# A linear-attention layer with a GELU MLP on one core: two loads under way from the fourth on, and a planner that reckons with 235 bytes per ns

## The chip, the cores and the metric

The kernel runs on one core of a Trainium2 chip. The metric is device time in microseconds (us) of one execution. Engines are named as the profile names them: PE is TensorE (PEld its weight loads), DVE is VectorE, ACT is ScalarE, POOL is GpSimd, SP is SyncE, which issues every DMA here.

## What is computed

An RWKV-like recurrence over 768 tokens, for 4 batches and 8 heads of size 48, followed by an MLP with GELU (384 to 2048 to 384) on the 3072 tokens.

```
for t in range(S):
    cur = einsum('bhd,bhe->bhde', u[None] * k[:, :, t], v[:, :, t])
    y[:, :, t] = einsum('bhd,bhde->bhe', r[:, :, t], state + cur)
    state = w[None, :, :, None] * state + einsum('bhd,bhe->bhde', k[:, :, t], v[:, :, t])
x = y.transpose(0, 2, 1, 3).reshape(B * S, H * D)
h = x @ w_in
out = (0.5 * h * (1 + erf(h / sqrt(2)))) @ w_out
```

## The kernel before

**Tiling.** The tokens are cut into 6 chunks of 128. In a chunk, two heads make a pair, so that there are 24 groups (chunk, pair), worked on one after the other, four to a chunk. The recurrence of a group becomes matrix products: scores of keys and queries (L473, into the PSUM buffer A), what the group adds to the state (the gains, L484, into UE), and the readout from the old state and from the group itself (L492 and L510, into Y). The result is split into a high and a low half (L573 on ACT, L574 on DVE) into xx, the input of the MLP, or x for the pair that comes first and is spread over the three others (L523). The MLP of a chunk is 16 steps, one for each block of 128 hidden units: three times three products into Hp (L657), GELU (L687), split into gh and gl (L688, L689), nine products into O (L700). 96 steps in all.

**Loads.** A group needs T (r and k with the head dimension on partitions, L252 and L254, 448 or 384 KB; from the third group on in two halves of 48 rows) and N (k and v by token, L261, 384 KB). T is multiplied by powers of the decay on DVE (L434), N on POOL (L441). The first four groups have buffers of their own, T0 to T3 and N0 to N3; the later ones take turns in Tb and Nb. The 16 blocks of weights (768 KB each, L372) land in three buffers raw in turn and are split into wh and wl in six passes on ACT and DVE (L387 to L400). All that happens in the first lap over the blocks; later chunks find the weights in place.

**What holds a load back.** Loads go through `in_turn` (L227), which keeps only so many of them under way. It makes each load wait, on SP, until the load `back` places before it in the list `landing` has landed. SP issues in order, so whatever stands behind a waiting load waits too.

```
back = UNDERWAY + (len(landing) < START)
behind = landing[-back] if first is not None and len(landing) >= back else None
```

The first thirteen stand in `LOADS`: t0, t1, n0, t2, n1, t3, w0, n2, n3, w1, t4, w2, n4, where t is T, n is N and w is a block of weights.

**The planner.** The kernel writes no order by hand. Each operation is added to a `Plan` (L52) with its engine, a duration, a due time, and what it reads and writes. `Plan.run` (L89) then steps through model time, picks the ready operation with the earliest due time on each engine, and emits it; each engine executes in the order emitted. A load of n bytes is reckoned as n / RATE ns on a bus that carries one load at a time, 1050 ns after its issue and 940 ns before its landing is seen.

```
if e == "sp":
    free[e] = start + 640
    bus = max(bus, start + 1050) + ns / RATE
    end = bus + 940
```

**Fillers.** Where the planner sees TensorE waiting in the prologue, it fills the gap with products of zeros that nobody reads (`heat`, L314, all recorded at L315): wide ones of 512 columns into UE or A, narrow ones of 256 columns into AE. How many are emitted follows from the gap in model time:

```
for _ in range(int(share * (start - free[e]) / ns)):
    fill()
```

They are ordinary instructions of TensorE's stream, and run whether the data came sooner or later than in the model. From the first group of the second chunk on none is emitted.

Of the kernel before, what the change touches and what calls it, by code (L numbers as in the profile page):

```python
# [34 lines left out]
WMIN, WMAX = 0.7, 1.25  # L35
NT = 8
NEAR = 8
RATE = 270.0
LATER = 10 ** 7
FIRST, STEP, STEP_LAST = 23000, 8400, 3900  # L40
WEIGHT_AHEAD, GROUP_AHEAD, GROUP_DUE = 12500, 28000, 20000
HEATS, SMALL, HEAT_NS, HEAT_ROOM = 7, 26, 400, 300
LOADS = ("t0", "t1", "n0", "t2", "n1", "t3", "w0", "n2", "n3", "w1", "t4", "w2", "n4")
UNDERWAY, START = 2, 10
URGENT, WORTH = 1000, .5
LEEWAY, SHARE = 700, 0.9
BARE = 2
# [4 lines left out]
class Plan:  # L52
# [26 lines left out]
    def time(self, n):  # L79
        e, ns = self.ops[n][:2]  # L80
        return 2200 + ns / RATE if e == "sp" else ns

# [6 lines left out]
    def run(self):  # L89
# [14 lines left out]
        for _ in self.ops:  # L104
# [28 lines left out]
# [4 lines that stand above are left out]
# [823 lines left out]
```

## Time and profile before

| what | us |
|---|---|
| three timed runs | 487.2, 490.36, 490.95 |
| their median | 490.36 |
| the profiled execution | 487.44 |
| its span, first to last instruction | 485.6 |
| TensorE busy in the span | 477.3 |
| VectorE, ScalarE, GpSimd busy | 266.0, 176.3, 63.7 |

How to read it: the profile is of one execution, whose own time is the span and some 2 us around it. Busy time is an average over a prologue of some 30 us (loads, masks, the first four groups), a first lap with the splitting of the weights, and the rest, where only the groups and the MLP run. A stage's limit is read from that stage.

### The profile page before, as it was taken

The numbers are of one execution on the slowest core, as the hardware profiler recorded it, in microseconds if no ns is written. First come the engines' busy times: TensorE is split into PE (matmuls) and PEld (weight loads), VectorE is DVE, ScalarE is ACT, GpSimd is POOL, SyncE is SP. The second block draws the span as 40 slices with busy tenths as digits, with TensorE's granted clock in tenths as the row PEclk, the third lists the DMA queues.
The fourth block names the chain that finished last, engine by engine and source line by source line (L and its number), as shares of the span: only waits on it lengthen the run. The fifth ranks groups of instructions, "written<-read, shape, count | busy, mean of one in ns | idle before, by whom it ended". The sixth has DMA issues, their size and how long they took to land.

```text
span 485.6 us, 11783 instructions
## 1 busy us (share of the span) xinstructions
PE 477.3 (98%) x5150; PEld 387.7 (80%) x5150; DVE 266.0 (55%) x432; ACT 176.3 (36%) x355; POOL 63.7 (13%) x85
## 2 busy tenths in 40 slices
PE   8899999999999999999999999999999999999996
PEld 5788778888887887888888878888888887888885
DVE  7888977983654556535536536545544422322223
ACT  6588978843122134222232331331431311211111
POOL 4200000002202202202022122022021100000000
PEclk9999999999999999999999999999999999999999
DMA  8776676331311312312302403113403000100002
GB/s 215 229 248 247 202 219 215 112 93 66 83 45 51 93 45 89 108 35 60 93 20 74 148 1 93 44 51 94 136 12 93 1 12 13 65 1 0 0 1 70
DMA packets 13193, 42.25 MB, mean 87 GB/s; under 512 B 2160, under 2 KB 2544, under 8 KB 13136
## 3 DMA queue, kind: packets, MB, share of 16 engines
q1 hardware_dynamic: 13136, 41.43, 28.4%
q8 instruction: 42, 0.69, 0.6%
q14 instruction: 15, 0.12, 0.1%
HBM read 34.74 MB, written 4.72 MB: 81 GB/s over the span
## 4 chain that ended last, share of the span: by engine, by line
PE 96%; DMA 1%; DVE 1%; issue 1%; SPq 0%; DVEq 0%
PE Hp L657 42%; PE O L700 41%; PE A L473 3%; PE Y L492 3%; PE Y L510 2%; PE Y L484 1%; PE AE L315 1%; PE Y L700 1%; DMA T<-in_rkT_dram 1%; PE Y L523 0%; DVE Am L559 0%; PE UE L484 0%; DVE wa L873 0%; DVE T L434 0%; PE A L315 0%
## 5 line engine op out<-in xcount | busy, mean ns | idle before, releaser
L657 PE MATMUL Hp<-xx,wh 128*128 128x512 f32 x576 | 166.7, 397 | 0.0
L687 ACT ACTIVATE gf<-Hp 128x512 f32<-128x512 f32 x96 | 57.4, 598 | 231.3 <-PE Hp L657 225.5
L688 DVE CAST gh<-gf 128x512 fp32r<-128x512 f32 x95 | 45.4, 478 | 170.8 <-ACT gf L687 170.0
L657 PEld LDWEIGHTS Hp<-xx,wh 128*128 128x128 f32 x576 | 106.8, 188 | 24.9 <-ACT gf L687 0.4
L657 PE MATMUL Hp<-xx,wl 128*128 128x512 f32 x288 | 83.3, 396 | 0.0
L700 PE MATMUL O<-gh,wh 128*128 128x512 f32 (+1 forms) x285 | 81.9, 394 | 0.0
L700 PE MATMUL O<-gh,wl 128*128 128x512 f32 (+1 forms) x285 | 80.9, 390 | 0.5 <-issue 0.5
L700 PE MATMUL O<-gl,wh 128*128 128x512 f32 (+1 forms) x285 | 80.5, 389 | 0.0
L689 DVE TENSOR_TENSOR gl<-gf,gh 128x512 fp32r<-128x512 f32 x95 | 73.5, 774 | 9.3
L657 PEld LDWEIGHTS Hp<-xx,wl 128*128 128x128 f32 x288 | 54.0, 188 | 12.9
L700 PEld LDWEIGHTS O<-gh,wh 128*128 128x128 f32 x285 | 52.4, 188 | 12.6 <-issue 0.3
L700 PEld LDWEIGHTS O<-gh,wl 128*128 128x128 f32 x285 | 52.5, 188 | 12.5 <-issue 0.9
L700 PEld LDWEIGHTS O<-gl,wh 128*128 128x128 f32 x285 | 52.6, 188 | 11.5
L464 ACT ACTIVATE Am<-diag,cs 128x64 f32<-128x64 f32 x120 | 31.7, 338 | 27.3 <-DVE cs L459 27.3
L438 POOL TENSOR_TENSOR Nb<-Nb 128x384 f32<-128x384 f32 x15 | 15.7, 1047 | 122.3 <-DMA Nb<-in_rkv_dram 114.7
L441 POOL TENSOR_TENSOR Nb<-Nb,WN 128x384 f32<-128x384 f32 x20 | 21.0, 1048 | 50.8 <-DMA Nb<-in_rkv_dram 30.1
L434 DVE TENSOR_TENSOR Tb<-Tb,E 112x1024 f32<-112x1024 f32 x20 | 24.3, 1215 | 3.1 <-DMA Tb<-in_rkT_dram 3.1
L529 DVE SCALAR_TENSOR_TENSOR Sb<-Sa,E,Y 48x192 f32<-48x192 f32 x40 | 16.5, 413 | 14.2 <-ACT xx L573 7.7
L501 POOL MEMSET turn<- 1x1 f32 x19 | 1.7, 88 | 137.3 <-PE Y L492 137.3
L573 ACT CAST xx<-Y 112x512 fp32r<-112x512 f32 (+1 forms) x18 | 10.6, 587 | 22.9 <-PE Y L484 16.4
L559 DVE COPY_PREDICATED Am<-past,A 128x512 f32<-128x512 uint32 x24 | 17.6, 735 | 0.4
L456 POOL TENSOR_TENSOR Nb<-Nb,u_sb 128x384 f32<-128x384 f32 x15 | 17.8, 1188 | 0.1
(112 smaller groups left out, 396.8 us busy)
## 6 DMA issues: line engine op xcount, KB each, us to landing
raw<-in_wmlp_dram SPq DMA_DIRECT2D x16, 768.0 KB, 5.0
Nb<-in_rkv_dram SPq DMA_DIRECT2D x15, 576.0 KB, 3.9
Tb<-in_rkT_dram SPq DMA_DIRECT2D x40, 192.0 KB, 3.5
out_dram<-raw SPq DMA_DIRECT2D x5, 768.0 KB, 3.7
Nb<-in_rkv_dram SPq DMA_DIRECT2D x5, 384.0 KB, 3.3
xx<-x SPq DMA_DIRECT2D x30, 64.0 KB, 2.3
N<-in_rkv_dram SPq DMA_DIRECT2D x4, 384.0 KB, 5.1
T<-in_rkT_dram SPq DMA_DIRECT2D x2, 448.0 KB, 4.7
```

Of the source, the lines that this page charges most:

```text
L434: add("dve", sdve(1024), LATER if g.gi else -10 ** 5, lambda: nc.vector.tensor_tensor(out=flat, in0=flat, in1=E[:, 0, g.p].rearrange("l h ...
L438: add("pool", pool(DM), LATER, lambda: nc.gpsimd.tensor_tensor(out=g.n[:, 0], in0=g.n[:, 0], in1=g.n[:, 1], op=ALU.mult), r=[g.K], w=[g.R])
L441: it = nc.gpsimd.tensor_tensor(out=g.kn, in0=g.kn, in1=WN[:, g.p].rearrange("s j d -> s (j d)").unsqueeze(1).to_broadcast([C, NB, 2 * D]), ...
L456: add("pool", pool(DM), LATER, lambda: nc.gpsimd.tensor_tensor(out=g.n[:, 0], in0=g.n[:, 0], in1=u_sb[:, g.p, :].unsqueeze(1).to_broadcast ...
L464: add("act", sact(HALF) + 60, LATER, lambda x=x, b=b: nc.scalar.activation(out=g.am[:, x, b, :], in_=diag2, func=AF.Copy, scale=g.sums[:, ...
L529: return nc.vector.scalar_tensor_tensor(out=g.s[h + 1][quarter(1 - x)], in0=g.s[h][l], scalar=E[l, 1, g.p, h, MID:MID + 1], in1=gained(g, ...
L559: add("dve", 722, LATER, lambda: nc.vector.copy_predicated(out=g.am, mask=mask.bitcast(U32).unsqueeze(1).unsqueeze(1).to_broadcast([C, 2, ...
L657: nc.tensor.matmul(O[3], lhsT=wt[j][:, 0, k_ * 128:(k_ + 1) * 128], rhs=x[:, a, k_, :], start=start and k_ == ks[0], stop=stop and k_ == k ...
L687: add("act", 600, LATER, lambda: nc.scalar.activation(out=gf, in_=O[3], func=AF.Gelu), r=["H"], w=["gf"])
L688: add("dve", sdve2(512), LATER, lambda: nc.vector.tensor_copy(out=high, in_=gf), r=["gf"], w=[GH])
L689: add("dve", sdve(512), LATER, lambda: nc.vector.tensor_tensor(out=low, in0=gf, in1=high.bitcast(F32), op=ALU.subtract), r=["gf", GH], w=[GL])
L700: nc.tensor.matmul(bank(dst)[:, a:b], lhsT=wt[j][:, 1, d * 128:(d + 1) * 128], rhs=gt[:, a:b], start=(j == 0 and n == 0), stop=(j == NJ - ...
```

## The change

Three numbers change: START, up to which three loads may be under way, goes from 10 to 3, RATE from 270 to 235 bytes per ns; UNDERWAY stays at 2. Since the first three loads never wait, the fourth is now the first to do so, and waits for the second load and no longer for the first.

```
--- before.py
+++ after.py
@@ -35,13 +35,13 @@
 WMIN, WMAX = 0.7, 1.25
 NT = 8
 NEAR = 8
-RATE = 270.0
+RATE = 235.0
 LATER = 10 ** 7
 FIRST, STEP, STEP_LAST = 23000, 8400, 3900
 WEIGHT_AHEAD, GROUP_AHEAD, GROUP_DUE = 12500, 28000, 20000
 HEATS, SMALL, HEAT_NS, HEAT_ROOM = 7, 26, 400, 300
 LOADS = ("t0", "t1", "n0", "t2", "n1", "t3", "w0", "n2", "n3", "w1", "t4", "w2", "n4")
-UNDERWAY, START = 2, 10
+UNDERWAY, START = 2, 3
 URGENT, WORTH = 1000, .5
 LEEWAY, SHARE = 700, 0.9
 BARE = 2
```

SP issues the same loads in the same order; what they wait for moves. On SP before (DMAHW1, 2, 3 and 5 tell the landing of T0, T1, N0 and of the second half of T2):

```order
L252 DMA T1_103<-in_rkT_dram 112x1024
L261 DMA N0_110<-in_rkv_dram 128x768
L254 DMA T2_104<-in_rkT_dram 48x1024 [waits DMAHW1_49,Pool_49]
L254 DMA T2_104<-in_rkT_dram 48x1024
L261 DMA N1_111<-in_rkv_dram 128x768 [waits DMAHW2_49]
L254 DMA T3_105<-in_rkT_dram 48x1024 [waits DMAHW3_49,Pool_49]
```

And on SP after:

```order
L252 DMA T1_103<-in_rkT_dram 112x1024
L261 DMA N0_110<-in_rkv_dram 128x768
L254 DMA T2_104<-in_rkT_dram 48x1024 [waits DMAHW2_49,Pool_49]
L254 DMA T2_104<-in_rkT_dram 48x1024
L261 DMA N1_111<-in_rkv_dram 128x768 [waits DMAHW3_49]
L254 DMA T3_105<-in_rkT_dram 48x1024 [waits DMAHW5_49,Pool_49]
```

T2 waits for T1 in place of T0, N1 for N0 in place of T1, T3 for T2 in place of N0; the loads up to the tenth follow in the same manner, and from the eleventh on each waits for the same load as before.

On PE, behind the gains of the first group (the first of the three numbers in a row is the buffer: T_102 to T_105 and N_110 to N_113 belong to groups 0 to 3, AE<-zeros are narrow fillers):

```order
 L484 MATMUL UE<-N_110 48x48 x16
-L315 MATMUL AE<-zeros 128x256 x13
+L315 MATMUL AE<-zeros 128x256 x10
+L473 MATMUL A<-T_104 64x64 x16
+L473 MATMUL A<-T_104,KB_108 64x64 x16
 L492 MATMUL Y<-T_102,Sb 48x64 x8
 L510 MATMUL Y<-Am_116,N_110 48x64 x16
-L473 MATMUL A<-T_104 64x64 x16
-L473 MATMUL A<-T_104,KB_108 64x64 x16
-L484 MATMUL UE<-N_111 48x48 x16
-L315 MATMUL AE<-zeros 128x256 x11
+L315 MATMUL AE<-zeros 128x256 x12
```

The scores of group 2 move ahead of the readout of group 0, and the gains of group 1 move behind the scores of group 3. Over the whole prologue the narrow fillers go from 13 + 11 + 12 + 12 = 48 to 10 + 12 + 6 + 17 + 10 = 55. On DVE the two selects of group 1 (L559) move with this, directly behind the product of T2 (L434) and ahead of the setting of the spread matrix (L306, L307).

On PE, in the first two steps of the MLP (wh_75 and wl_83 are the two halves of the weights of step 0, wh_76 those of step 1; A<-zeros are wide fillers):

```order
 L657 MATMUL Hp<-xx_122,wl_83 128x512
 L657 MATMUL Hp<-xx_122,wh_75 128x512
-L315 MATMUL A<-zeros 128x512
+L315 MATMUL A<-zeros 128x512 x5
 L657 MATMUL Hp<-xx_122,wh_75 128x512
 L657 MATMUL Hp<-xx_122,wl_83 128x512
 L657 MATMUL Hp<-xx_122,wh_75 128x512
-L315 MATMUL A<-zeros 128x512 x3
+L315 MATMUL A<-zeros 128x512 x5
 L657 MATMUL Hp<-xx_122,wh_76 128x512 x3
```

The wide fillers there go from 1 + 3 to 5 + 5. One more wide filler, into UE, stands before the gains of the first group. Further on the planner swaps neighbours on ACT, DVE and PE: in the first lap ACT takes its three passes over block 4 (L390, L387, L393) before it makes the high half of block 3 (L398), as before, but now with its last pass over block 3 (L387) ahead of them all. POOL's order is unchanged.

## Rows read from the trace of the kernel before

**Rows 1.** The page: busy times, granted clock by slice, chain by engine.

```profile
PE 477.3 (98%) x5150; PEld 387.7 (80%) x5150; DVE 266.0 (55%) x432; ACT 176.3 (36%) x355; POOL 63.7 (13%) x85
...
PEclk9999999999999999999999999999999999999999
...
PE 96%; DMA 1%; DVE 1%; issue 1%; SPq 0%; DVEq 0%
```

**Rows 2.** Busy time by stretch: us, engines' busy us, clock, DMA share, GB/s.

```profile
34.04:160.00 125.96, 125.49 (x1580) 101.72 (x1581) 90.69 (x144) 74.03 (x123) 14.46 (x20) 1.00 0.43 134
```

**Rows 3.** Chain in order of time, 12 to 34 us: start us, us, what.

```profile
12.21 1.74 PE AE L315 x13
...
16.42 0.61 issue
...
17.73 1.51 PE AE L315 x11
...
21.36 0.70 issue
...
23.59 1.62 PE AE L315 x12
...
27.38 1.63 PE AE L315 x12
...
32.42 0.23 PE A L315
```

**Rows 4.** Timeline of SP, 5 to 36 us: start us, us, engine, what.

```profile
5.47 0.79 SPq L254 DMA_DIRECT2D T<-in_rkT_dram  x2
7.06 0.35 SPq L261 DMA_DIRECT2D N<-in_rkv_dram  x1
...
34.30 1.59 SPq L372 DMA_DIRECT2D raw<-in_wmlp_dram  x2
```

**Rows 5.** DMA issues at 5.8, 49, 7, 32.6 and 34.3 us: KB, us to landing.

```profile
T<-in_rkT_dram SPq DMA_DIRECT2D x1, 192.0 KB, 4.2
...
Tb<-in_rkT_dram SPq DMA_DIRECT2D x1, 192.0 KB, 3.3
...
N<-in_rkv_dram SPq DMA_DIRECT2D x1, 384.0 KB, 6.0
...
Nb<-in_rkv_dram SPq DMA_DIRECT2D x1, 384.0 KB, 2.9
...
raw<-in_wmlp_dram SPq DMA_DIRECT2D x1, 768.0 KB, 5.0
```

**Rows 6.** Timeline of VectorE (DVE), 10 to 16 us.

```profile
10.53 1.96 DVE L434 TENSOR_TENSOR T<-T,E 112x1024 f32<-112x1024 f32 x1
...
13.17 0.73 DVE L559 COPY_PREDICATED Am<-diag,A 128x512 f32<-128x512 uint32 x1
13.94 0.73 DVE L559 COPY_PREDICATED Am<-past,A 128x512 f32<-128x512 uint32 x1
14.56 1.21 DVE L434 TENSOR_TENSOR T<-T,E 112x1024 f32<-112x1024 f32 x1
```

**Rows 7.** DMA queues from 14.4 to 14.6 us: packets, MB, share of 16 engines.

```profile
q1 hardware_dynamic: 20, 0.05, 88.6%
q8 instruction: 1, 0.02, 33.9%
```

**Rows 8.** Timeline of ScalarE (ACT), 39 to 45 us.

```profile
39.35 0.92 ACT L390 ACTIVATE wb<-raw 128x768 uint32<-128x768 uint32 x1
...
40.96 1.07 ACT L393 ACTIVATE wb<-raw 128x768 f16<-128x768 f32 x1
41.90 0.87 ACT L387 ACTIVATE wa<-raw 128x768 f32<-128x768 f32 x1
44.06 0.83 ACT L398 CAST wh<-wa 128x768 fp32r<-128x768 f32 x1 [1.29 <-DVE wa L395]
```

**Rows 9.** Timeline of TensorE (PE) at 46.6 us, the step on block 3.

```profile
46.62 0.97 PE L657 MATMUL Hp<-xx,wh 128*128 128x512 f32 x3
```

More of the change, by code (lines that the diff above doesn't have):

```diff
@@ L37 @@
 NEAR = 8
-RATE = 270.0
+RATE = 235.0
 LATER = 10 ** 7
@@ L43 @@
 LOADS = ("t0", "t1", "n0", "t2", "n1", "t3", "w0", "n2", "n3", "w1", "t4", "w2", "n4")
-UNDERWAY, START = 2, 10
+UNDERWAY, START = 2, 3
 URGENT, WORTH = 1000, .5
```

## The prediction

> **What bounds the kernel now.** I read the page first. TensorE is busy 98% of the span and is 96% of the chain that ended last, and the granted clock stands at its upper level in all forty slices [rows 1]. Then I cut the span into stretches. From 34.04 us, where the second MLP step begins, to 160 us TensorE works 125.49 of 125.96 us [rows 2]: there is nothing to win in the lap over the sixteen weight blocks, and a load that comes later there is hidden as long as its slack lasts. The change can act in the first 34 us and, if weights come late, in that lap.
>
> The chain in order of time shows what the first 34 us are made of [rows 3]. From 12.21 us on it never leaves TensorE: scores, gains and readout of four groups, and between them products of zeros ("AE L315", "A L315"). Those are the fillers, put where the planner expected TensorE to wait: 48 of 256 columns in the chain (13, 11, 12 and 12), and 4 of 512 columns. TensorE waits for nothing that the profile names there, except that it stands still twice, 0.61 and 0.70 us, called "issue", in the middle of a batch. The fillers are thus not free: in this execution nothing arrived later than they ended, and each moves the end by its own length.
>
> **The change part by part.** *Fillers.* With loads of 235 bytes per ns and two under way the planner expects later data, and writes 55 narrow fillers in place of 48, and 10 wide ones in place of 4. A narrow one costs (1.74 + 1.51 + 1.62 + 1.63) / 48 = 0.135 us, a wide one 0.23 us [rows 3]. Seven and six of them: 0.95 + 1.38 = 2.3 us. If the data really come as late as the planner thinks, TensorE would have stood still for that time, so the price is the same either way. One more wide one, into UE, stands earlier, where VectorE's first selects are waited for; that wait hides it, and it costs 0.23 us at most if not.
>
> *T2.* Before, SP issues T2 at 5.47 us, when T0 has landed; now it waits for T1, the landing that let N1 go at 7.06 us [rows 4]. Its second half is issued some 0.4 us behind the first and took 4.2 us; a half like it took 3.3 us with less beside it, at 49 us [rows 5]. T2 so lands at 10.8 to 11.6 us, against 10.0 us. VectorE took T2 up at 10.53 us, and needed 1.96 us where the next product of the same size took 1.21 us [rows 6]. I reckon 1.2 us, and behind it the two selects of group 1, 1.5 us (13.17 us to 14.67 us in the rows), which now follow at once, with the setting of the spread matrix behind them. They free the buffer A for the scores of group 2, which TensorE now does before it reads out group 0. Ready: 13.5 to 14.4 us. TensorE comes there at 12.21 us plus ten fillers, 13.56 us. Wait: 0 to 0.9 us; I take 0.5, the middle, as both durations of a half are equally near.
>
> *What is queued behind T2 on SP.* N1 goes behind N0, T3 behind T2, the first weight block behind N1, N2 behind T3, N3 behind the block, the second block behind N2, and SP issues in this order, so each may hold the next. N1 took 6.0 us with three under way [rows 5]; issued at about 8 us it lands by 14.1 us, and its gains now stand behind the scores of group 3. T3, of the same two halves as T2, has the same bounds of 0 to 0.9 us for the scores of group 3, but twelve fillers (1.62 us) stand ahead of those; I take 0.2. The first block goes some 2 us later, and its first product comes after the last narrow fillers, which end at 29.0 us: hidden. Without that cover the chain would lengthen by those 2 us.
>
> *The two stretches of "issue".* An instruction packet of queue q8 starts 1.9 us before the first of them, beside load packets that fill the DMA engines to nine tenths [rows 7]. With two loads under way it has less to queue behind, and more fillers stand between the batches of small products that eat instructions fastest. The two could shrink to nothing, or stay: 0 to 1.31 us back, I take 0.7.
>
> The Trainium skill (Runtime: NRT & Kernel Launch, Instruction fetch mechanics) says that instructions are refilled in blocks of 256 by a queue of their own and that this is mostly hidden. By that rule there would be nothing to give back here, and the sum would be 0.7 us higher. The trace agrees that such packets come on a queue of their own, and shows 1.31 us for which it names nothing else, so I keep the term.
>
> *Weights in the first lap.* For block 3, ScalarE ends the high half at 44.06 + 0.83 = 44.89 us [rows 8] and TensorE starts the step at 46.62 us [rows 9]: 1.7 us of slack, and TensorE itself will come about 2 us later. I cost the lap at nothing; this slack is the cover, and the third rival is the price without it. It can pay 0.47 us at most, TensorE's idle time there [rows 2].
>
> **The sum** is 2.3 + 0.5 + 0.2 - 0.7 = +2.3 us. Its ends are 2.3 - 1.31 = +1.0 us, and 2.3 + 0.9 + 0.9 = +4.1 us. On the profiled execution, 487.44 us (485.6 us of it span), that is 489.7 us. The timed runs of before stand at 487.2, 490.36 and 490.95 us: the median is 2.9 us above the profiled one, and no row tells why. From the median the same sum gives 490.36 + 2.3 = 492.7 us. I put the forecast midway between the two, 491.2 us. Its own range goes from 487.44 + 1.0 = 488.4 us to 490.36 + 4.1 = 494.5 us.
>
> [...]
>
> **Rivals.** First, *the stretches of "issue" go and nothing waits*: +1.0 us, 488.4 us from the profiled execution and 491.4 us from the median, 489.9 us between. For it: the packet lies where the DMA engines are full. Against it: batches of small products now stand closer, the scores of group 2 directly before the readout of group 0.
>
> Second, *the 2.9 us between the profiled execution and the median are late loads*. The old planner reckons with 270 bytes per ns; where loads run slower, TensorE waits behind its fillers, and the new plan has that time filled already. Then after stands at 489.7 us whatever the loads do: 0.7 us below the median. Nothing in the one trace speaks for or against it; it is why the forecast is not the full 492.7 us.
>
> Third, on the other side, *the weight blocks become the bound of the first lap*: slower. ScalarE's order puts three passes of block 4 (0.92 + 1.07 + 0.87 us) ahead of the high half of block 3 (0.83 us) [rows 8], so that block 3 is ready 3.7 us behind the landing of block 4, which was at 34.30 + 5.0 = 39.3 us [rows 4, 5]. The step on block 3 would start at 46.62 + 2.3 = 48.9 us, so the mechanism decides from a landing later than 45.2 us, 5.9 us later than before. Thirteen loads stand ahead, each behind the one two places before it; in one strand of six or seven, 0.9 us lost at each handover would do it, where a lone load takes 2.9 us whole. From there each further block waits for its own load: 0.5 us a step over the remaining twelve is 6 us, half of it hidden by the three buffers, so 491.2 + 3 to 491.2 + 6, say 495.8 us. Against it: from the eleventh load on the old kernel has two under way as well, and keeps its 1.7 us.
>
> Fourth, *faster by over 1%*: 4.9 us are wanted, and all that TensorE stands still between 12 and 160 us is 1.31 + 0.47 us. No row bears it out.
>
> **How the numbers follow.** Forecast 0.52, first rival 0.20, second 0.15, third 0.10, fourth 0.03. About 1%, that is 485.5 to 495.3 us around 490.36 us, is what a measurement of this kernel can tell from no change. Forecast and the first two rivals lie inside; of the third I count 0.02 inside. So faster 0.03, within 0.89, slower 0.08. The range 488.4 to 494.5 us holds the first two rivals too, and leaves out the third and the fourth and a little at both ends.
>
> **What would show it.** Right: the second MLP step starts 1 to 4.1 us later than 34.04 us; 55 and 10 fillers stand in a chain that is still all TensorE; a wait of under 1 us before the scores of group 2, with T2 landing at 10.8 to 11.6 us; and from the second step to the end as long as before, 485.6 - 34.04 = 451.6 us. Wrong: a chain that leaves TensorE for a load between 14 and 34 us, idle time of TensorE over 1 us between 34 and 160 us, or longer stretches of "issue".

## The result, and the profile after

The changed kernel takes 497.21 us (median of six runs, 492.45 to 503.13), the kernel before 488.34 us beside it (six runs, 487.07 to 490.95): a ratio of 1.014 [1.0105, 1.0175], slower by 1.4%, and above the predicted range. The ratios here are taken from fast executions alone, so that this one leaves out the run of 503.13 us, and they are not the quotients of the medians beside them. Timed again with more runs of before on one chip (the first experiment) it was 495.36 (four runs) against 489.76 us, 1.0129 [1.0085, 1.0172].

The profiled execution is the fastest of the six, 492.45 us, with a span of 490.7 us, 5.1 us longer than before's. The page, against [rows 1]:

```profile
PE 479.9 (98%) x5164; PEld 389.9 (79%) x5164; DVE 266.3 (54%) x432; ACT 176.4 (36%) x355; POOL 63.6 (13%) x85
...
PEclk9999999999999999999999999999999999999999
...
PE 94%; DMA 3%; issue 1%; DVE 1%; SPq 0%; ACT 0%
```

TensorE has 14 matmuls more, and loads are now 3% of the chain. The chain in order of time, against [rows 3] (start us, us, what):

```profile
7.52 4.37 DMA T<-in_rkT_dram
...
12.31 4.46 DMA T<-in_rkT_dram
...
21.67 0.72 PE AE L315 x6
...
24.08 2.23 PE AE L315 x17
...
28.48 1.38 PE AE L315 x10
...
33.26 1.14 PE A L315 x5
...
35.10 1.14 PE A L315 x5
36.24 2.10 PE Hp L657 x9
```

Up to 16.8 us the chain is the loads of T, one behind the other: T2's second half lands at 7.52 + 4.37 = 11.89 us, T3's at 16.77 us. The second MLP step begins at 36.08 us (its first matmul; the chain shows it one batch later), 2.0 us later than before. TensorE's stops and waits over the whole span:

```profile
PE Y L484 <- issue: 2.7, 1, 2.7
PE A L473 <- DVE Am L559: 2.1, 3, 0.8
PE A L315 <- DVE E L338: 1.6, 1, 1.6
PE Hp L657 <- ACT gf L687: 0.3, 1, 0.3
```

The third row stands in both kernels, at the very start. The second holds the waits for T2 and T3, through VectorE's selects. In TensorE's timeline (start us, us, what, and in brackets the idle time ahead and what ended it):

```profile
14.68 0.69 PE L473 MATMUL A<-T 48*64 48x64 f32 x32 [0.78 <-DVE Am L559]
...
19.48 0.69 PE L473 MATMUL A<-T 48*64 48x64 f32 x32 [0.82 <-DVE Am L559]
...
65.19 0.52 PE L484 MATMUL Y<-Nb 64*48 64x48 f32 x26
68.43 0.30 PE L484 MATMUL Y<-Nb 64*48 64x48 f32 x6 [2.72 <-issue]
```

The two stretches of "issue" of 0.61 and 0.70 us [rows 3] are gone. In their place stands one of 2.72 us in the first lap, in the middle of a batch of small products. The lap as a stretch, against [rows 2]:

```profile
36.08:160.00 123.92, 120.88 (x1439) 97.30 (x1438) 89.51 (x141) 71.94 (x117) 14.38 (x19) 1.00 0.45 137
```

TensorE is idle for 123.92 - 120.88 = 3.04 us there, against 0.47 us before. From the second step to the end it takes 490.7 - 36.08 = 454.6 us, against 451.6 us. So of the 5.1 us, 2.0 come ahead of the second step and 3.1 behind it. Of the latter, 2.25 us are that one stop, less the 0.47 us that before stood still, and 0.3 us a wait for ScalarE (the last row of the waits above); the rest has no wait to its name.

**Where the stop stands.** Before's 0.47 us of idle time in the lap is a stop called "issue" too, at another place of the work:

```profile
65.74 0.50 PE L700 MATMUL O<-gh,wl 128*128 128x512 f32 x1 [0.47 <-issue]
```

The two look unrelated until one counts. TensorE's matmuls in stretches that end within a stop, before (the number behind x is the count):

```profile
0.00:16.60 16.60, 14.00 (x348) 10.86 (x349) 13.01 (x27) 10.26 (x23) 6.11 (x14) 1.00 0.85 230
16.60:21.60 5.00, 4.33 (x127) 3.83 (x127) 4.07 (x8) 4.08 (x7) 1.99 (x2) 1.00 0.89 273
21.60:65.50 43.90, 42.94 (x765) 35.09 (x764) 37.38 (x55) 36.77 (x55) 3.38 (x5) 1.00 0.68 225
```

And after:

```profile
0.00:67.00 67.00, 61.38 (x1240) 50.47 (x1241) 52.01 (x84) 49.42 (x80) 11.69 (x21) 1.00 0.72 222
```

Before stood still behind matmul 348, 348 + 127 = 475 and 475 + 765 = 1240; after stood still behind 1240 as well. 765 is six times 127.5. The stops are tied to the number of the instruction, not to the work: TensorE stands where its stream passes from one block of some 127 matmuls with their weight loads to the next. The 14 extra matmuls at the start push all later work 14 places on in these blocks. In before, the last block ahead of no. 1240 runs from 61.42 to 65.27 us and holds 3.85 us of work, wide matmuls among it. In after it lies wholly within the 160 small products of a group, and is through in 2.0 us, from 63.72 to 65.71 us. The DMA queues of after from 63.72 us, when that block was entered, to 66.10 us, and in the tenth of a microsecond behind it (packets, MB, share of 16 engines):

```profile
q1 hardware_dynamic: 132, 0.74, 86.7%
...
q1 hardware_dynamic: 8, 0.02, 106.9%
q8 instruction: 1, 0.02, 60.1%
```

Until 66.10 us there is no instruction packet at all, beside loads that fill the engines to 87%. It comes 2.4 us after the block was entered, when TensorE has already stood for 0.4 us, and TensorE goes on 2.3 us after it. In before the packet came 2.0 us after the block was entered, and 3.85 us of work covered all but 0.47 us (the queues from 61.42 to 63.38 us, and from there to 63.50 us):

```profile
q1 hardware_dynamic: 74, 0.45, 76.6%
...
q8 instruction: 1, 0.02, 50.4%
```

### The profile page after: what moved, and what is told of

Same layout as the page of the kernel before. It is cut to its first block, busy times and chain, and to the rows that moved or that the text cites. A ratio compares the mean times of both kernels' runs of the same rounds, so it can differ in the third digit from the quotient of the medians.

```text
span 490.7 us, 11809 instructions
## 1 busy us (share of the span) xinstructions
PE 479.9 (98%) x5164; PEld 389.9 (79%) x5164; DVE 266.3 (54%) x432; ACT 176.4 (36%) x355; POOL 63.6 (13%) x85
## 4 chain that ended last, share of the span: by engine, by line
PE 94%; DMA 3%; issue 1%; DVE 1%; SPq 0%; ACT 0%
PE Hp L657 41%; PE O L700 40%; DMA T<-in_rkT_dram 3%; PE Y L492 3%; PE A L473 3%; PE Y L510 2%; PE Y L484 2%; PE Y L700 1%; PE AE L315 1%; PE A L315 0%; PE Y L523 0%; DVE Am L559 0%; DVE wa L873 0%; DVE T L434 0%; PE UE L484 0%
## 5 line engine op out<-in xcount | busy, mean ns | idle before, releaser
L700 PEld LDWEIGHTS O<-gl,wh 128*128 128x128 f32 x285 | 52.5, 188 | 11.6
L700 PEld LDWEIGHTS O<-gh,wl 128*128 128x128 f32 x285 | 52.5, 188 | 11.6
L434 DVE TENSOR_TENSOR Tb<-Tb,E 112x1024 f32<-112x1024 f32 x20 | 24.3, 1216 | 3.4 <-DMA Tb<-in_rkT_dram 3.3
L559 DVE COPY_PREDICATED Am<-past,A 128x512 f32<-128x512 uint32 x24 | 17.7, 739 | 0.5
```

Source lines behind the costliest of these rows:

```text
L434: add("dve", sdve(1024), LATER if g.gi else -10 ** 5, lambda: nc.vector.tensor_tensor(out=flat, in0=flat, in1=E[:, 0, g.p].rearrange("l h ...
L559: add("dve", 722, LATER, lambda: nc.vector.copy_predicated(out=g.am, mask=mask.bitcast(U32).unsqueeze(1).unsqueeze(1).to_broadcast([C, 2, ...
L700: nc.tensor.matmul(bank(dst)[:, a:b], lhsT=wt[j][:, 1, d * 128:(d + 1) * 128], rhs=gt[:, a:b], start=(j == 0 and n == 0), stop=(j == NJ - ...
```

## The experiments

The theory: the time goes where a block of instructions is run through faster than the next one is fetched, and the change moved small products into such a place. The rivals: the 17 fillers and the late T2 and T3 cost it (*fillers*), or one of the two edits by itself does, by its loads. To move the places without moving anything else, the number SMALL of tiny warm-up products (L323) was changed; each is two matmul records, of about 20 ns, that feed nothing. There the planner's price of the warm-up was set to its old value, so that the plan stays word for word the same:

```
-        add("pe", 430 * HEATS + 40 * SMALL, 10, warm_up, ...
+        add("pe", 4050, 10, warm_up, ...
```

The table gathers what was measured. "Places" is by how many matmuls the work stands further on than in before. "Step 2" is where the second MLP step begins in the profiled execution, "lap on" the time from there to the end. Stops are those called "issue" of over 0.4 us, with the number of matmuls ahead of them.

| run | places | median us (before) | ratio | step 2 | lap on | stops: no. and us |
|---|---|---|---|---|---|---|
| before | 0 | 488.34 | | 34.04 | 451.6 | 348 0.61, 475 0.70, 1240 0.47 |
| after | +14 | 497.21 (488.34) | 1.014 | 36.08 | 454.6 | 1240 2.72 |
| again | +14 | 495.36 (489.76) | 1.0129 | 38.99 | 454.9 | 602 1.45, 1240 2.57 |
| after_fewer_small | 0 | 491.38 (489.76) | 1.0031 | 37.52 | 452.8 | 1240 0.68 |
| before_more_small | +14 | 491.87 (489.76) | 1.0059 | 37.37 | 452.0 | 348 0.48, 475 2.07, 602 1.18, 1240 0.95 |
| start_only | +2 | 489.34 (489.76) | 1.0016 | 35.63 | 451.3 | 348 0.58 |
| rate_only | +4 | 493.02 (489.52) | 1.0084 | 37.77 | 453.3 | 602 1.10, 1240 1.38 |
| after_half_fillers | 0 | 490.92 (489.52) | 1.0039 | 34.27 | 457.4 | 348 0.43, 1240 3.35 |
| after_small14 | -10 | 491.12 (489.52) | 1.0059 | 35.86 | 455.1 | 348 0.67, 984 2.67 |
| before_small21 | -10 | 489.31 (489.52) | 1.0005 | 33.14 | 451.0 | none |
| start_small32 | +14 | 491.27 (489.7) | 1.0036 | 37.05 | 452.9 | 368 1.99, 475 0.44, 1240 1.37 |
| rate_small24 | 0 | 492.02 (489.7) | 1.0031 | 38.54 | 452.7 | 475 0.49, 602 1.01, 1240 0.70 |
| after_small33 | +28 | 494.99 (489.7) | 1.0095 | 40.45 | 453.3 | 1496 1.51 |
| before_half_fillers | -10 | 490.23 (488.42) | 1.0031 | 35.84 | 451.5 | 984 0.41 |

Of these 26 stops, 25 stand on the ladder, and each of the 25 ends 2.2 to 2.8 us after the start of an instruction packet in its own trace. The one behind no. 368 does not: the last such packet started 5.3 us before it ended. "Step 2" needs care: in six of the profiles (start_only, rate_only, after_fewer_small, rate_small24, after_small33, before_half_fillers) TensorE's products go at a slower pace until 10 to 17 us, in the other eight only until 5 to 6 us (*Other places* below).

### The changed kernel again, and its places moved back

`again` is the changed kernel unaltered.

> The changed kernel once more, unaltered, for a second profile. Theory of the instruction blocks: TensorE stands still for about 2.7 us at its matmul 1240, near 68 us, as in the first profile, and the second MLP step starts about 36.2 us. Rival theory (the stop at 68 us was an accident of one execution): the stop is gone or stands at another matmul. The timed runs of the changed kernel lie 3 to 10 us above its profiled one with a mean granted clock of 0.993 to 0.997; if the clock falls behind TensorE's waits, a profile of such a run shows a clock below 1.0 behind a wait, and if the loads are merely slower it shows later landings at full clock.

`after_fewer_small`, 14 matmuls fewer:

```
-HEATS, SMALL, HEAT_NS, HEAT_ROOM = 7, 26, 400, 300
+HEATS, SMALL, HEAT_NS, HEAT_ROOM = 7, 19, 400, 300
```

> The changed kernel with 19 in place of 26 tiny warm-up products, which run while TensorE waits for the first load, and with the planner's numbers as they were: all later matmuls stand 14 places earlier in the instruction stream, as in the kernel before. Theory of the instruction blocks: the stop at matmul 1240 falls from 2.7 to about 0.5 us, at a place near 68 us that is 14 matmuls further on in the work; span about 488.5 us, 2.2 us under the changed kernel's 490.7. Rival theory (the stop comes from loads that are late there): the stop stays at the same products, 2.7 us, span 490.7 us.

Beside the same 25 runs of before, the changed kernel measured 495.36 us (1.0129 [1.0085, 1.0172]), and with its places moved back 491.38 us (1.0031 [1.0003, 1.0058]): 4.0 of the 5.6 us are gone, with loads, fillers and plan as in the change. The profiled span fell by less than expected, to 490.3 us: its second step begins 1.4 us later than in after's first profile, though TensorE waits for neither T2 nor T3 there; this is one of the profiles with the slow pace at the start. The stop at no. 1240 came again in the one, 2.57 us, and in the other shrank to about before's size, at before's place in the work:

```profile
69.93 0.39 PE L700 MATMUL O<-gh,wl 128*128 128x512 f32 x1 [0.68 <-issue]
```

`again` shows a second loss. Its second step begins at 38.99 us, not near 36.2 us as expected. It has one more stop, of 1.45 us behind no. 602, and the granted clock after it stands at 0.50, the lower of TensorE's two levels, for 3.41 us (stretches that end in the two stops, then the stretch behind the first and the next one; the clock is the third number from the end):

```profile
0.00:28.00 28.00, 23.98 (x602) 19.59 (x602) 20.37 (x39) 16.25 (x33) 8.22 (x16) 1.00 0.70 197
0.00:70.00 70.00, 63.20 (x1240) 51.78 (x1241) 51.79 (x84) 49.36 (x80) 11.47 (x21) 0.98 0.70 213
...
29.00:32.41 3.41, 3.40 (x60) 3.31 (x61) 1.75 (x4) 2.37 (x5) 0.63 (x1) 0.50 0.74 218
32.41:34.00 1.59, 1.50 (x27) 1.22 (x30) 1.59 (x2) 1.43 (x2) 0.39 (x1) 1.00 0.96 398
```

Half the clock for 3.41 us is 1.7 us of work, or a mean granted clock of 0.996 over the span. By the clocks listed with each timed run, 0.997 or less occurs in 8 of 10 executions of the changed kernel, in 28 of 93 of before, and in none of 10 with the places moved back. It is no mark of the places alone: `before_more_small` and `start_small32` (14 on) have 4 of 10 each, but so has `after_half_fillers` at before's places.

### Before, with its places moved forward

```
-HEATS, SMALL, HEAT_NS, HEAT_ROOM = 7, 26, 400, 300
+HEATS, SMALL, HEAT_NS, HEAT_ROOM = 7, 33, 400, 300
```

> The kernel before with 33 in place of 26 tiny warm-up products and nothing else changed: all later matmuls stand 14 places further on in the instruction stream, as in the changed kernel. Theory of the instruction blocks: the stop of 0.47 us near 65.7 us becomes about 2.7 us in the middle of the gains of a group, span 485.6 + 2.2 = about 488 us. Rival theory (late loads): nothing changes, 485.6 us.

491.87 us, 1.0059 [1.0029, 1.009]: 2.1 us more than before in the same job, from products that feed nothing, and 14 of which take 0.3 us at the pace of before's own (52 in 1.00 us). TensorE's waits of the profiled execution, the three rows of "issue":

```profile
PE A L473 <- issue: 2.5, 2, 2.1
...
PE Y L510 <- issue: 1.2, 1, 1.2
PE Y L484 <- issue: 1.0, 1, 1.0
```

All at numbers of the same ladder (348, 475, 602, 1240). The stop at no. 1240 stands in the small products, as in after, but is only 0.95 us long: the place decides where a stop can come, not how long it is.

### The two edits apart

The change is of two numbers, START and RATE (UNDERWAY stays at 2). `start_only` and `rate_only` each undo one of the two edits:

```
-RATE = 235.0
+RATE = 270.0
```

```
-UNDERWAY, START = 2, 3
+UNDERWAY, START = 2, 10
```

> Half of the change: two loads under way from the fourth on, planner still at 270 bytes per ns. Its fillers are 48 narrow ones and 6 wide ones (before 48 and 4, changed kernel 55 and 10). Theory of the fillers: second MLP step about 0.5 us later than before by the fillers, plus 0 to 2 us of waits for T2 and T3 that no filler covers, so at 34.6 to 36.5 us. Theory of the loads alone: waits of 0.8 us before the scores of group 2 and of group 3 as in the changed kernel, whatever the planner thinks. If TensorE's waits bring the clock down, its runs show a clock under 1.0 as those of the changed kernel do.

> The other half of the change: planner at 235 bytes per ns, three loads under way up to the tenth as before. Fillers 45 narrow and 10 wide in the chain and one more wide one into UE, so that the later matmuls stand 4 places further on in the instruction stream than in the kernel before (14 in the changed one). Theory of the instruction blocks: the stop at matmul 1240 is 0.47 + 4 x 0.23 = about 1.4 us, where the changed kernel has 2.6 to 2.7. Theory of the fillers: 6 x 0.23 - 3 x 0.135 = 1.0 us more on TensorE, second MLP step near 35 us. Both together: about 2 us above the kernel before, 491.5 us. Rival (the two halves work only together, late loads behind a plan that fits them): no difference from the kernel before, 489.8 us.

The load limit alone costs nothing that can be measured: 489.34 us, 1.0016 [0.999, 1.0042], although T2 and T3 set out as late as in the change. The waits for them that were expected do not stand in its profile, where the slow pace at the start lasts until 10.2 us. The planner's 235 alone, with each load waiting for the same one as before, costs 493.02 us, 1.0084 [1.0054, 1.0114]: +3.5 us, where 2 were expected. So later loads by themselves are not what makes the change slow; the plan is, by what it writes or by the places that it gives the rest. In `rate_only` the work stands 4 places on, and the stop at no. 1240 is 1.38 us.

### The two edits apart, with the places set

`start_small32` puts the first of these 14 places on, `rate_small24` the second back to before's places (SMALL 32 and 24, with the edits above).

> Two loads under way from the fourth on, planner at 270 bytes per ns, and 32 in place of 26 tiny warm-up products, so that the later matmuls stand where they stand in the changed kernel (14 places further on than before). Theory of the instruction blocks: the stop at matmul 1240 becomes 2.6 to 2.7 us in the middle of the gains of a group, and the median about 2.5 us above the version with 26 (489.3 us): 491.5 to 492 us. Rival (the stop belongs to the planner's 235): no such stop, 489.3 us.

> Planner at 235 bytes per ns, three loads under way up to the tenth, and 24 in place of 26 tiny warm-up products, so that the later matmuls stand where they stand in the kernel before. Theory of the instruction blocks: the stop at matmul 1240 falls from 1.38 to about 0.5 us, so 0.9 us under the version with 26 (493.0 us): 492.1 us; what is left over 489.5 us is fillers and waits of the prologue. Rival (the fillers alone make it slow): 493.0 us.

`start_small32`: 491.27 us, 1.0036 [1.0011, 1.0061], against 1.0016 for the same kernel unmoved. Two stops of size have come; the second is the one at no. 1240, as in after, but half as long. The first stands behind no. 368, 20 matmuls past the rung, the only stop of over 0.4 us that is off the ladder, and no instruction packet starts shortly before its end; what it waited for stays open:

```profile
PE UE L484 <- issue: 2.0, 1, 2.0
...
PE Y L484 <- issue: 1.4, 1, 1.4
```

`rate_small24`: 492.02 us, 1.0031 [1.0003, 1.006], against 1.0084. The stop at 1240 fell from 1.38 to 0.70 us, the others (602, 475) stayed. Setting the places from before's to after's or back thus acts with the same sign in all four plans: by the ratios +0.6% on before, -1.0% on after, -0.5% on the planner's edit (4 places), and +0.2% on the load limit (12 places); in the last two the intervals overlap. And both kernels with the new plan and the old places keep the same 0.3%, whichever load limit they have; it is just clear of no difference.

### Fewer fillers

SHARE is the part of an expected wait that the planner fills. In `after_half_fillers` 29 narrow and 6 wide fillers stand in place of 55 and 10, with SMALL 34 to bring the places to before's; in `before_half_fillers` (on before) 26 and 2 in place of 48 and 4, with SMALL 33:

```
-LEEWAY, SHARE = 700, 0.9
+LEEWAY, SHARE = 700, 0.5
```

> The changed kernel with the share of a gap that is filled cut from 0.9 to 0.5: 29 narrow and 6 wide fillers in the chain in place of 55 and 10, and 34 tiny warm-up products in place of 26, so that all later matmuls keep the places of the version with 19 of them (491.4 us). Theory of the fillers, as predicted: each is on the path, 26 x 0.135 + 4 x 0.23 = 4.4 us less, second MLP step near 33 us, 487 us. Rival: the data come as late as the planner thinks, so that TensorE waits as long as it worked on fillers: 491.4 us, with 3 to 4 us of waits that name VectorE or ScalarE between 13 and 36 us. Second rival: with fewer fillers the granted clock stands at half level longer, so slower than 491.4 us.

> The kernel before with the share of a gap that is filled cut from 0.9 to 0.5 (26 narrow and 2 wide fillers in place of 48 and 4) and 33 in place of 26 tiny warm-up products, so that the later matmuls stand 10 places earlier than before, where the profile had no stop after the prologue. Theory of the fillers, as predicted (nothing comes later than they end): 22 x 0.135 + 2 x 0.23 = 3.4 us less, 486 us. Rival (most of them stand where data are late anyway): 0 to 1 us less, 488.5 to 489.5 us, with waits that name VectorE or ScalarE in the first 34 us. Second rival (TensorE with fewer fillers stays at half clock longer in the prologue): slower than before.

Both speak against fillers that each cost their own length. In the changed kernel the second step begins 1.8 us earlier than in after's first profile, where the fillers' length promised 4.4, and the time, 490.92 us, is only 0.5 us below `after_fewer_small`, beside other runs of before; by the ratios (1.0039 against 1.0031) it is no faster. In before, where 3.4 us were to be won, it became 490.23 against 488.42 us, 1.0031 [1.0008, 1.0053]: slower. Its chain now leaves TensorE (start us, us, what), and TensorE waits where it never did:

```profile
13.87 1.99 DVE T L434
...
25.48 0.59 ACT xx L573
26.09 0.70 DVE xx L574
...
34.24 0.99 ACT wb L393
35.23 0.56 ACT gf L687
```

With fewer fillers the data are awaited. But this profile differs from before's in one more thing, named beforehand as the second rival: its slow pace at the start lasts until 13.5 us, before's until 4.9 us. The same 32 score products of the first group (before, then `before_half_fillers`):

```profile
8.20 0.69 PE L473 MATMUL A<-T,KB 48*64 48x64 f32 x32
```

```profile
11.17 1.11 PE A L473 x32
```

The first product behind VectorE's selects so begins at 14.02 us, against 10.69 us, ahead of any narrow filler. From there to the second step it takes 21.82 us, against 23.35 us, and 1.0 of these 1.5 us are shorter stops of "issue". So in the profiles 24 fillers of 3.4 us gave back some 0.5 us: most of them had been lying on time that would have been lost anyway. Why the median rose by 1.8 us isn't settled by this. By the clocks listed, 7 of its 12 executions have a mean granted clock of 0.997 or less (down to 0.991), against 3 of the 17 of before beside them, so the slower clock remains a rival.

`after_half_fillers` also shows the largest stop, behind no. 1240 again. That block was entered at 62.45 us, and the instruction packet comes 4.8 us later (first the DMA queues from 62.45 to 67.25 us, and from there to 67.40 us; then the stretches up to the stop, and from 70.80 us, 1.1 us behind it):

```profile
q1 hardware_dynamic: 263, 1.46, 83.5%
...
q8 instruction: 1, 0.02, 40.5%
```

```profile
0.00:68.00 68.00, 61.27 (x1240) 49.02 (x1241) 55.65 (x90) 52.56 (x86) 12.57 (x21) 1.00 0.72 226
...
70.80:74.20 3.40, 3.40 (x9) 2.62 (x8) 0.16 (x1) 0.00 (x0) 0.00 (x0) 0.50 0.44 113
74.20:76.00 1.80, 1.80 (x9) 1.46 (x8) 0.79 (x2) 1.52 (x3) 0.43 (x1) 0.99 0.27 109
```

Its places are before's, so a good place is no insurance: when the packet is late enough, 3.85 us of work don't cover it either.

### Other places

`after_small14` and `after_small33` move the changed kernel to -10 and +28, `before_small21` moves before to -10 (SMALL 14, 33 and 21, edited as above).

> The changed kernel with 14 in place of 26 tiny warm-up products: later matmuls stand 24 places earlier in the instruction stream than in the changed kernel, 10 earlier than in the version with 19. Theory of the instruction blocks: the stop at matmul 1240 is gone (0.7 - 10 x 0.23 is below nothing), other stops may move in; 490.5 to 491.5 us. Rival (the version with 19 was better because of fewer warm-up products, not because of places): better or worse in step with their number, so 488.5 us or, if they warm the clock, 494 us.

> The changed kernel with 33 in place of 26 tiny warm-up products: later matmuls stand 14 places further on than in the changed kernel. Theory of the instruction blocks: the block that begins at matmul 1113 now begins inside the group's small products by 14 places less of the work before them, so its stop stays at 2.6 us, and other blocks come to begin just ahead of such products; 0 to 6 us above the changed kernel (495.4 us). Rival (more warm-up products keep the clock up or cost nothing): 495.4 us, with the same stops.

> The kernel before with 21 in place of 26 tiny warm-up products: later matmuls stand 10 places earlier. Theory of the instruction blocks: the stop of 0.47 us at matmul 1240 goes, the two in the prologue move by ten small matmuls and keep about their size; 0 to 0.5 us under the kernel before, 489.3 to 489.8 us. Rival (number of warm-up products alone): 33 of them cost 2.1 us, so 21 give back 1.5 us, 488.3 us.

`after_small14`: 491.12 us, 1.0059 [1.0025, 1.0094], 4.2 us under `again`, though against another set of before. The stop at 1240 is gone. Another stands two rungs lower, behind no. 984, where now a batch of the same small products ends the block, with the clock at 0.50 for 3.4 us around and behind it:

```profile
50.22 0.57 PE L484 MATMUL Y<-Nb 64*48 64x48 f32 x15 [2.67 <-issue]
...
50.00:53.40 3.40, 3.18 (x21) 2.41 (x21) 1.90 (x4) 2.55 (x5) 0.00 (x0) 0.50 0.68 168
```

`before_small21`: 489.31 us, 1.0005 [0.9974, 1.0036], no gain. Its profiled execution has no stop of over 0.4 us and is the shortest span of all, 484.2 us, but its ten runs reach from 486.08 to 492.48 us.

`after_small33` is a miss for a theory of the one stop. No stop stands at 1240, the largest is 1.51 us behind no. 1496, and it still takes 494.99 us, 1.0095 [1.0064, 1.0126]. In its profile the time is lost ahead of the second step, at 40.45 us. There the products themselves are slow: the four wide warm-up products took 2.07 us, where before's took 1.19 us. The two rows, of this kernel and of before:

```profile
6.89 2.07 PE L315 MATMUL UE<-zeros 128*128 128x512 f32 x4
```

```profile
5.79 1.19 PE L315 MATMUL UE<-zeros 128*128 128x512 f32 x4
```

Products go at the slower pace until 16.6 us in this execution, until 14.5 us in `after_fewer_small`, 10.2 us in `start_only`, 4.9 us in before's, while the clock's column reads 1.00 in all of them. That column is no evidence here: the trace's list of granted clocks has its first entry at just these times (16.60, 14.47, 10.25 and 4.92 us), and the column reads 1.00 where no entry stands. Ahead of the first entry, products of 512 columns begin every 0.43 us, behind it every 0.23 us. In the stretch of `after_half_fillers` from 70.80 us that is listed at 0.50 they begin every 0.43 us too, so the slow pace at the start is that of the lower level. The slow pace is in executions of both loads' orders, and one profile of each kernel doesn't tell whether the change makes it more frequent.

No version beat the kernel before.

## Why the prediction was wrong, and where it was right

**The term that failed: "The two stretches of issue", sized at 0 to 1.31 us back.** The mechanism was the right one, packets of a queue of their own that come too late, and these two stretches did go in the profiled execution. But I sized it from the two stops that stood there, as something local to the loads of the first 34 us, and gave it only a gain. A stop belongs to a rung of the instruction count. Fourteen matmuls more move every later batch against that ladder, in the lap too, and there the 160 small products came to lie in front of a rung: +2.25 us (2.72 - 0.47) in the profile. So the term that I put at -0.7 us was -1.31 us in the prologue and +0.94 us over the span. The rule weighed there from the Trainium skill (Runtime: NRT & Kernel Launch, Instruction fetch mechanics) has the blocks right: 127 to 128 matmuls with as many weight loads are 254 to 256 instructions. That crossing a block is mostly hidden holds by count: after passes some 40 such bounds and stands still for longer than 0.2 us at only one of them. But a single stop is up to 3.35 us long here.

**The step that follows from it: "I cost the lap at nothing", with 451.6 us from the second step to the end "as long as before".** It was 454.6 us, and idle time of over 1 us between 34 and 160 us was the sign that I had named for being wrong. The cover that I had named, the slack of the weight blocks, held but for 0.3 us of waiting for ScalarE; the loss came mostly from what no weight block has a part in.

**The range was built on one execution.** The clock at 0.50 behind some of the stops was in no term. At some 1.7 us a time, with a mean clock of 0.997 or less in 8 of 10 executions of the changed kernel, it can be 1.5 to 2 of the 4.8 us by which its median lies above its own profile; the rest isn't explained. And the reading that the clock stood at its upper level in all forty slices of [rows 1] holds only from 4.92 us on, where the list of clocks begins.

**Right: the size of the first 34 us.** The second step begins 2.04 us later, forecast +2.3 (1.0 to 4.1). The waits for T2 and T3 are 0.78 and 0.82 us, inside 0 to 0.9, where I took 0.5 and 0.2. T2 landed at 11.89 us, just past my 10.8 to 11.6, since its second half went off at 7.52 us and took 4.37 us; VectorE's product on it took 1.23 us, as reckoned (1.2). But that the sum came out is partly luck: waits and "issue" were each off by 0.6 to 0.9 us, in opposite directions.

**Wrong, though hidden in that sum: "each moves the end by its own length".** Leaving out 24 fillers of before made it slower, not 3.4 us faster, and in its profile gave back some 0.5 us.

**The rivals.** The weight blocks did not become the bound of the lap: those 0.3 us are all that TensorE waited there for anything but instructions in the first profile of the change, and 0.8 us in `again`. The time that this rival named, 495.8 us, is near the measured one, but by luck. Late loads as the reason of the 2.9 us between before's profile and its median: not borne out, since the plan with 235 makes the kernel slower with either load limit. So the slower side was priced by the wrong mechanism.

**What stays open.** Of the 1.3%, 1.0% goes with the 14 places, and 0.3% stays with the new plan (`after_fewer_small` and `rate_small24`, 1.0031 both). How much of that is fillers and how much waiting wasn't separated, and the two kernels with fewer fillers don't do it, since clock and stops differ there too. `after_small33` shows that stops alone don't order all the medians: the slow pace at the start can weigh as much. Why the packet comes 2 us after a block's entry in one execution and 4.8 us in another was not tried. Before's own trace points to the transfers beside it: if the ladder is carried on by 127.5 matmuls, blocks are entered at 139.6 and 175.7 us with no DMA packet under way, and their instruction packets start 0.5 and 0.8 us later, against 2.0 us ahead of no. 1240.

## What to carry to other kernels

A change that adds a handful of instructions early moves everything behind it against the blocks in which instructions are fetched. So count instructions at each stop called "issue", and if the counts form a ladder, look at what the change puts in front of each rung: dense batches of small matmuls ahead of a rung leave the least time to cover the next block. Before one believes a plan or a load limit to be the cause, shift the stream by a few products that feed nothing and time it again: here that alone was worth up to 4.0 us of 490. And look where the list of clocks begins before comparing the first microseconds of two profiles.

## What the runs showed of the hardware that had not been expected

- Stops of TensorE at fixed numbers of its own instructions (348, 475, 602, 984, 1240, 1496; one, behind 368, apart), whatever work stands there. All but that one of the 26 end 2.2 to 2.8 us after the start of an instruction packet. At no. 1240 their size went from nothing to 3.35 us.
- Behind some stops the granted clock is 0.50 for about 3.4 us (after 1.45, 3.35 and 2.67 us of standing; around the stop of 1.99 us behind no. 368 too), behind others it stays at 1.00: after the 2.72 us of the changed kernel the stretch from 68.40 to 72.00 us has

```profile
68.40:72.00 3.60, 3.57 (x20) 2.91 (x20) 3.19 (x5) 2.78 (x5) 0.00 (x0) 1.00 0.06 20
```

- At the start the same four wide products take 1.19 us in some executions and 2.07 us in others, for a time that ended between 4.9 and 16.6 us. The clock's column reads 1.00 there, because the list of granted clocks begins only when that time is over; the pace is that of the lower level.
